# Another order for the instructions of a two-layer attention and feed-forward kernel, with a changed planner constant

## The chip, the cores and the metric

The kernel runs on one core of a Trainium2 chip. The metric is the device time of one execution in microseconds (us), lower is better. A core has engines that run side by side: PE (TensorE, matmuls), DVE (VectorE), ACT (ScalarE), POOL (GpSimd) and SP (SyncE, which here only issues transfers); PEld is the loading of a matmul's stationary operand. Transfers are issued from SP's and POOL's instruction queues, and each queue is worked through in order.

## The reference

The input x has 2048 rows of 512. Four stages follow one another, each added to its input after a layer norm: attention, feed-forward, attention, feed-forward, both times with the same weights.

```python
for s in range(n_seg):                       # 64 segments of 32 rows, one after the other
    h = concat([mem, xs])                    # 8 memory rows and 32 rows of the segment: 40
    q, k, v = h @ Wq, h @ Wk, h @ Wv         # 32 heads of 128
    p = softmax(where(mask, q @ k.T * scale, -1e9))
    o = (p @ v) @ Wo
    mem = o[:8]                              # the next segment needs it
    outs.append(o[8:])
...
h = sigmoid(x @ w_gate) * (x @ w_up)         # 512 to 1792
return h @ w_down
```

The memory rows make the segments of one attention stage a chain: a segment cannot begin before the output projection of the one before it.

## The kernel before

The program is first written down as a list of 13442 tasks and then emitted in an order that a string holds. `Kern.trace` (L1098) makes the list: after the start (weights loaded, the first blocks of x normed, their values computed by `v_pass` and `v_half` and stored to the DRAM tensor `scr`) come 70 calls of `emit_step` (L740). Step t does segment t of the first attention stage and segment t - 6 of the second, side by side in the same matmuls (80 columns, 40 of each; fewer in the first 6 and the last 6 steps). A step goes through the 32 heads in groups of six (three pairs):

- q and k (L817): 8 matmuls a head; ACT copies them to `qku` (L838);
- scores (L852), softmax on DVE and ACT (L866 to L883), transpose (L895), copies to `ptsb` (L909);
- product with the values (L922). The values come by transfer into the tile `vsb`, of which there are three, two in use by a step: rows computed early are read back from `scr` (L786), and the rows that need the memory are computed in the step itself as strips (L731), copied to `sst` and sent to `vsb` (L797). All of these are SP's, 16 or so a step, and a `vsb` is free again only after the products that read it;
- the output projection (L940); DVE writes the memory rows into the next step's input (L953, L958).

Between these PE does a feed-forward (`ffn`, L995) of 128 rows every fourth step for each stage: gate and up (L1042), tanh, down (L1065). Its weights do not fit, so they stream: `wg`, `wu` and `wd` tiles in rings of three, each 256 KB, loaded by POOL (L1034, L1035, L1059).

The class `Planner` (L178) sets the order. `add` (L202) gives each task its engine (or two that can do it), its assumed duration and latency, and what it reads and writes. `plan` (L239) decodes `SEQUENCE`: for every task its place among those not yet taken, then one bit for each of the 1573 tasks that two engines can do. Each engine then runs its tasks in that order. `replay` (L258) goes through the order once with assumed times, and three things of it reach the program: which buffer of a pool a task gets, where gaps foreseen in PE's time are filled with placeholder matmuls on zeros (`warm`, L322; emitted at L1159), and the pacing of the weight loads: a big transfer of POOL is given a matmul that has to end before it starts, the last one whose planned end lies `PACE` = 465 ns before the load's planned start (L295 to L300).

In `replay` a task starts when its engine is free and all that it waits for is done, with a latency on top: for a wait on PE 205 ns (`LAT`), and 32 ns more (`TO_PE`) if the waiting task is PE's (`gap`, L232, and the reuse of buffers, L285). The constant `TO_POOL` = 0 stands there (L183) but nothing reads it. The search that finds a sequence is not part of the kernel.

Of the kernel before, what the change touches and what calls it, by code (L numbers as in the profile page):

```python
# [1238 lines left out]
```

## Time and profile before

| what | value |
|---|---|
| median of 3 timed runs | 1776.29 us (1774.72 to 1777.69) |
| profiled execution, its own time | 1771.19 us |
| its span, first to last instruction | 1769.4 us |
| busy PE, PEld, DVE, ACT, POOL | 1750.3, 1507.4, 1228.8, 1113.9, 572.4 us |
| q and k matmuls (L817), two rows | 614.9 and 615.1 us |
| output projection (L940) | 367.8 us |
| gate and up (L1042), two rows | 172.1 and 171.4 us |
| placeholder matmuls (L1159) | 19.5 us, 69 of them |
| POOL's weight loads, issue to landing | 4.3, 4.3 and 4.1 us (median) |
| moved by DMA | 273.42 MB, 155 GB/s; 299 GB/s in the first 50 us |

The page gives busy times and the share of the span; PE's matmuls overlap, and their ends are modelled. A row of waits names who waited for whom, the total in us, how often, and the longest. In the chain that ended last, each line is a piece of time with its start and length and what it was spent on: work of an engine, a queue's issuing (SPq), or a transfer from issue to landing (DMA out<-in).

### The profile page before, as it was taken

How to read it: one execution, taken by the hardware profiler on the slowest of the kernel's cores; microseconds unless marked ns; L12 is line 12 of the kernel's file. 1: busy time of each engine (PE TensorE's matmuls, PEld its weight loads, DVE VectorE, ACT ScalarE, POOL GpSimd, SP SyncE). 2: the span in 40 equal slices, each digit the busy share in tenths (PEclk: the TensorE clock that was granted, in tenths of full speed). 3: DMA queues.
4: the chain of work that ended last, by engine and by line, in shares of the span. 5: the costliest groups of instructions: out<-in, count | busy, mean ns of one | idle time of the engine just before them, and what ended most of it. 6: DMA issues, size and time to landing. Idle time of an engine off the chain costs nothing.

```text
span 1769.4 us, 92147 instructions
## 1 busy us (share of the span) xinstructions
PE 1750.3 (99%) x40043; PEld 1507.4 (85%) x40043; DVE 1228.8 (69%) x4104; ACT 1113.9 (63%) x2938; POOL 572.4 (32%) x823
## 2 busy tenths in 40 slices
PE   9999999999999999999999999999999999999999
PEld 4588888889888888989898898988888898989887
DVE  5577777677667666776676777667767766767676
ACT  4576766667666656666665567666656666666654
POOL 5212032413333242323333242333325132342423
PEclk9999999999999999999999999999999999999999
DMA  9834355645555464545545554555547354554644
GB/s 316 294 96 133 96 168 148 190 113 155 151 148 151 141 181 134 169 117 161 155 141 158 140 173 127 149 160 161 161 124 209 110 159 116 155 171 121 185 128 117
DMA packets 135600, 273.42 MB, mean 155 GB/s; under 512 B 30754, under 2 KB 68522, under 8 KB 135194
## 3 DMA queue, kind: packets, MB, share of 16 engines
q0 software_dynamic: 55920, 180.99, 34.8%
q1 hardware_dynamic: 79274, 86.53, 16.9%
q8 instruction: 314, 5.14, 1.2%
q14 instruction: 92, 0.75, 0.1%
HBM read 221.78 MB, written 27.07 MB: 141 GB/s over the span
## 4 chain that ended last, share of the span: by engine, by line
PE 91%; DMA 4%; SPq 2%; DVE 1%; issue 1%; ACT 0%; POOL 0%; DVEq 0%; POOLq 0%; ACTq 0%
PE bank L817 32%; PE bank L940 17%; PE bank L1042 11%; PE bank L731 7%; PE bank L606 6%; PE bank L1065 5%; PE bank L922 4%; PE bank L852 4%; PE bank L895 2%; PE bank L566 1%; DMA wo_sb<-in_A_Wo_dram 1%; SPq L797 1%; DMA oxT<-in_A_x_dram 1%; DMA scr<-wg 1%; DMA vsb<-scr 1%
## 5 line engine op out<-in xcount | busy, mean ns | idle before, releaser
L817 PE MATMUL bank<-hT,wk_sb 128*128 128x80 bf16 (+3 forms) x8960 | 614.9, 198 | 3.7 <-issue 2.1
L817 PE MATMUL bank<-hT,wq_sb 128*128 128x80 bf16 (+3 forms) x8960 | 615.1, 198 | 0.7 <-issue 0.4
L1173 ACT CAST qku<-bank 128x480 bf16<-128x480 f32 (+3 forms) x770 | 381.6, 507 | 236.0 <-PE bank L817 208.4
L817 PEld LDWEIGHTS <-wq_sb 128*128 128x128 bf16 x8960 | 453.0, 99 | 27.5 <-issue 13.1
L817 PEld LDWEIGHTS <-wk_sb 128*128 128x128 bf16 x8960 | 447.0, 99 | 2.7 <-DMA wk_sb<-in_A_Wk_dram 1.7
L866 DVE TENSOR_TENSOR st<-bank,cst 40x240 f32<-40x240 f32 (+3 forms) x768 | 280.1, 368 | 152.9 <-PE bank L852 140.1
L940 PE MATMUL bank<-otsb,wo_sb 128*128 128x80 bf16 (+1 forms) x8960 | 367.8, 198 | 0.9 <-DMA wo_sb<-in_A_Wo_dram 0.9
L940 PEld LDWEIGHTS <-wo_sb 128*128 128x128 bf16 x8960 | 337.8, 99 | 12.8 <-DMA wo_sb<-in_A_Wo_dram 1.3
L1173 ACT CAST otsb<-bank 128x480 bf16<-128x480 f32 (+3 forms) x420 | 201.5, 482 | 97.9 <-PE bank L922 69.5
L1059 POOL DMA_DIRECT2D wd<-in_B_w_down_dram x217 | 154.0, 710 | 311.3 <-PE bank L1065 110.8
L1035 POOL DMA_DIRECT2D wu<-in_B_w_up_dram x217 | 164.7, 759 | 256.0 <-PE bank L1042 82.9
L1034 POOL DMA_DIRECT2D wg<-in_B_w_gate_dram x217 | 164.1, 757 | 248.8 <-PE bank L1042 122.9
L876 ACT ACTIVATE st<-st 80x240 f32<-80x240 f32 (+3 forms) x420 | 159.6, 382 | 67.8 <-DVE st L873 64.8
L1042 PE MATMUL bank<-xnT,wg 128*128 128x128 bf16 (+2 forms) x1784 | 172.1, 219 | 1.2 <-DMA wg<-in_B_w_gate_dram 1.1
L1042 PE MATMUL bank<-xnT,wu 128*128 128x128 bf16 (+2 forms) x1784 | 171.4, 218 | 0.0
L878 DVE TENSOR_REDUCE small<-st 80x6 f32<-80x240 f32 (+3 forms) x420 | 151.1, 361 | 24.9 <-ACT st L876 22.3
L852 PE MATMUL bank<-qku 128*128 128x80 bf16 (+1 forms) x2240 | 162.7, 198 | 0.9 <-ACT qku L1173 0.9
L873 DVE TENSOR_TENSOR st<-st,small 80x240 f32<-80x240 f32 (+3 forms) x420 | 154.9, 371 | 6.6
L883 DVE TENSOR_TENSOR pb<-st,small 80x240 bf16<-80x240 f32 (+3 forms) x420 | 153.7, 370 | 6.0
L871 DVE TENSOR_REDUCE small<-st 80x6 f32<-80x240 f32 (+3 forms) x420 | 151.7, 363 | 6.0
L922 PE MATMUL bank<-ptsb,vsb 104*128 104x80 bf16 x2048 | 140.6, 199 | 3.9 <-DMA vsb<-scr 2.8
L556 POOL TENSOR_TENSOR small<-small,cst 128x1 f32<-128x1 f32 (+1 forms) x80 | 46.2, 578 | 301.8 <-DVE small L555 299.9
(107 smaller groups left out, 2412.5 us busy)
## 6 DMA issues: line engine op xcount, KB each, us to landing
wg<-in_B_w_gate_dram POOLq DMA_DIRECT2D x220, 256.0 KB, 4.3
wu<-in_B_w_up_dram POOLq DMA_DIRECT2D x220, 256.0 KB, 4.3
wd<-in_B_w_down_dram POOLq DMA_DIRECT2D x220, 256.0 KB, 4.1
vsb<-scr SPq DMA_DIRECT2D x460, 48.0 KB
vsb<-sst SPq DMA_DIRECT2D x464, 32.0 KB
scr<-vst SPq DMA_DIRECT2D x112, 96.0 KB
wv_sb<-in_A_Wv_dram SPq DMA_DIRECT2D x8, 512.0 KB
wo_sb<-in_A_Wo_dram SPq DMA_DIRECT2D x10, 384.0 KB
```

Of the source, the lines that this page charges most:

```text
L817: nc.tensor.matmul(o_ap, lhsT=W[:, c, h * P:(h + 1) * P], rhs=mv(c), start=(c == 0), stop=(c == DC - 1))
L852: nc.tensor.matmul(s_all(SB)[:, w0 + i, :], lhsT=fview(qku[:, i, 0, 0:1], [(1, P)]), rhs=qku[:, i, 1, 0:ncol], start=True, stop=True)
L866: pl.add("DVE", dve_ns(n, True), lambda gsz=gsz, hs=hs, st=st, SB=SB, pj_=pj_, npj_=npj_, mk=mk, idx=idx: nc.vector.tensor_tensor(out=st[p ...
L873: pl.add("DVE", dve_ns(n), lambda gsz=gsz, hs=hs, st=st, mx=mx: nc.vector.tensor_tensor(out=st[pr, hs], in0=st[pr, hs], in1=mx[pr, hs].uns ...
L876: pl.add("ACT", act_ns(n), lambda hs=hs, st=st: nc.scalar.activation(out=st[pr, hs], in_=st[pr, hs], func=ACTF.Exp, scale=self.scale), r=s ...
L922: nc.tensor.matmul(fview(OB[:, o:o + 1], [(ncol, 2), (1, L)]), lhsT=self.vsb[halves[u // 8]][0:64 + L, j, (u % 8) * P:(u % 8 + 1) * P], rh ...
L940: nc.tensor.matmul(WB[:, c * ncol:(c + 1) * ncol], lhsT=self.wo[:, h, c * P:(c + 1) * P], rhs=otsb[:, hl, 0:ncol], start=(h == 0 and c == ...
L1034: pl.add("POOL", 760, lambda wg=wg, fs=fs: nc.gpsimd.dma_start(out=wg[:], in_=self.wgv[:, :, fs]), r=[("wo", self.H - 1)], w=[gk] + bt, la ...
L1035: pl.add("POOL", 760, lambda wu=wu, fs=fs: nc.gpsimd.dma_start(out=wu[:], in_=self.wuv[:, :, fs]), r=[("wo", self.H - 1)], w=[uk] + bt, la ...
L1042: nc.tensor.matmul(gu[:, 2 * i + k, 0:n], lhsT=W[:, c, i * P:(i + 1) * P], rhs=xnT[:, c, rw], start=(c == 0), stop=(c == DC - 1))
L1059: pl.add("POOL", 760, lambda wd=wd, ip=ip: nc.gpsimd.dma_start(out=wd[:], in_=self.wdv[:, 2 * ip:2 * ip + 2, :]), w=[dk] + (["boot"] if se ...
L1173: nc.scalar.copy(out=dst, in_=src)
```

## The change

Two things change. First, the planner: `TO_POOL` becomes 257, and a new method reads it, so that in the planned times a task of POOL that waits for PE counts 257 ns more.

```diff
-    TO_PE, TO_POOL, PACE = 32.0, 0.0, 465.0
+    TO_PE, TO_POOL, PACE = 32.0, 257.0, 465.0
...
-        return a.lat + d + (self.TO_PE if b.eng[0] == "PE" else 0.0)
+        return a.lat + d + self.over(a, b)
+
+    def over(self, a, b):
+
+        return self.TO_PE if b.eng[0] == "PE" else self.TO_POOL if a.eng[0] == "PE" and b.eng[0] == "POOL" else 0.0
...
-                        t = max(t, ready(T[u], tk, 0.0 if same else T[u].lat + (self.TO_PE if tk.eng[0] == "PE" else 0.0)))
+                        t = max(t, ready(T[u], tk, 0.0 if same else T[u].lat + self.over(T[u], tk)))
```

Second, all lines of `SEQUENCE` are others (85 before, 84 after, some 14,000 characters). The tasks, what they depend on and what they compute stay; their order on each engine and the engine of some copies change:

| read out of the two strings | before | after |
|---|---|---|
| tasks on PE | 4202 | 4202 |
| tasks on DVE | 4100 | 4132 |
| tasks on ACT | 2937 | 2905 |
| tasks on POOL | 812 | 814 |
| tasks on SP | 1391 | 1389 |

Of the 1573 tasks that two engines can do, 530 change engine. PE's order differs mostly in where pieces of the feed-forward, values and scores lie between the projections of a step; in 50 of the 70 steps the last output projection has the same matmuls' work ahead of it within 0.05 us. In SP's and POOL's queues the transfers of a burst stand in another order.

More of the change, by code (lines that the diff above doesn't have):

```diff
@@ new lines @@
+@_r#~~-gm}MW;UejiWp{aJ)hi+l<6Ygrtd;7TKwO!xBySu(XZCrMjF7u`VA8t(jR!J{zR48z@Aiz$Lx>u=+Da|Nd@Jl@C!f9e6$s2{=Bom3p1|oAKY+p+<pV&Q?LU`v_4TZTh(Y*7k{uTw~)t889>{(ro!SoMr>PYU15#msZ
+_}t+ek9rur<9#IIr?bpIJH!kkm1`@DI$;_#upVyKMH=^*}z36l&bjqmxJr<2*;@Y&`>sORISXA?*4Kh9}6>clU~Q*(Ztx-1Jo^LiJ>2)99=JGEZs{pR9wj?m6fv{5u6yJ=7B^Cg2-DU*XDS*q4ueJ*wl#L0OuF3gnn2@I2W|
+I|9NbCrGR{Jip%xBqiFuV!Bf$3M6;LjF=W~UJH<g7`i1VZsE@R51DQH=IuLCb0}H4MUuI$tk4{EQMv@7i|pXc7{od_bJ!Z;@A?LZUj6-~nJg^Vw(q5xhy>fv4)%eRgl;}7W1feO6xvgFOVo@{Q<g$S!T41ZYWD8X{RWev3Zy
@@ new lines @@
+Ryh1AKtZJ}*M_d~*clQv!?_O(LhFXy4^Qy{g%b)re${{`K14VW+80jW^+%|bLlIPN{3#$&3*iV$hcYnMKO!1J+2V2B1-?Nwzxa@r+Mm#a>F?%b_X0C(3ljxJ!j7@`4ot+NL;c>g(MRO9?aJFC3a2Ho_!g$sV{WYL?Dkal!XV
+@+^^eEU8<s#XnQjX*dw-{8J<gnvo|+_`w`?W7wu&vlEO%YqB(OaA}fFr87cMohwR1MpZ^*xOT0#NJhLsn&T>0d5v<eo!!}8XV9CdnF=U9mjeEnL!4(d7yZ_ybuRghPRU61x0_vQN?a;z1ZW7fSPMM?R0|&Xal0odTIy)MUXz
+!bvxg-Ou0A5;&?tJxBc#?w=~3THxeKX1EHJ+?AzCG1r?&dIc$K9BsxIj9Zcc#LFncBB%GRpQ)KxBVCx|g-ENCrklW{MH*^IEXc_4`1V-jREC${Q3`gH*^=;P7?|&0H+hM>-HkZ{W%ztPn=z^-pEI7t?>6h+vGqOr6Rvuy4ft
@@ new lines @@
+40nPc@$uPvEosQ2Y|)nIKXK&rh{I&Uox}Xp@l}ND@z;eQp@H`^4M?0si?|>FM7a?7yYnOurV4#EoGevdai_XMK~SBs;eeQ5~(9z-V({bt18AG~n!isTDl8Msk-c0ADjgC0C3*@Lwuq0C>(sD}rOMj{g`;D(bSEs)wuVmckUp
+47ma*F*bKwFl>YscB(?TVKo(g3kksEi%iB^E1;z@>i7Q%vz8u+FW?iy<}5d+I3sgF%xP^!tZnw|V-q;3=hAT82qj4r&re;vxN)T-GCRM$yI3WX!~7VHvgH!`8$?Y}G%kFMxT7_r*m89mwn(T&iKVdqcbmG|hgSzj_5|g{OJc
+R(5d9!S3u|k+d&!DQb-K44Pe7Y`5o#evpE&KVqp*p4myYjmV`Gd3d{OPFkFJ*f=l;RVz1IB+&uXZK%RxX1!}UsW5X1gnspCdb`l4k*4T(kICd;vH3Zyr~Eq5|)@v=}{IAR{b+8@TVaS$JT+H&`VT<A*-9$4)n2zyJt+TqV^%
@@ new lines @@
+&r8W@^zu2WI>;NZiq15vYQx0;<C)fwd-H1a-`+j`h7}-l3x1|C9g`OGsFGRJN2yvDUU^Kx7u%@nR*J!6forss36zR+~{<;1WM(#<emy&6Jk$&m?iDL7Tt1<*)QN?B0mQ~3gQ+tNr{~(0b`g4<9N<DmOQEtE9G?A&A9q@Z3+`
+#@HHeP5*_V#W%tQF#8^3A@APVUvQb0w=$uax&HuCqWt{+-5wWpr4@v{s-GYDc^^df-s41ZzUxpa{uQtm>FNGR!{g5n-VUB|x2@eZC>;+ubkKjE3D>|FuN;&;f@@Zs4MwdCIwVhk#=2eawi%w8jh$O(XZ{5TJk!25T4pgdm#m
+zm54B6Y{`mGUuXP3*KW0w-P)f)#nXX@|I%cdQTW4tUYmtjn`()Uj3zf4HoC=Em|0y~KitYRDX24EI`drN7z>9+(;&Q^CzHl1#J=;DP{?QfsTEI+}7I3^z#zt>mq>j>+t_?66QS1nXMY@Ad_=HTt2jFm8~wA60Dvbny8*u3CN
@@ new lines @@
+8XmnU?X+LwX3ui2zXnF`bSu+yn5T>7>HT2<GC(Z5pXRTMs8w`PC)?$nA`3?3oz-KmdaQ(;env^f8ps5q7lkRR14}KCC_Mn2jAAn>TdiihS&6`L!3u_e6IYY62rL=CFm`8@T(gS^rBAYX<|x~<2RPtw`4{~KQOJ5GHc$W}Y`i
+RRZg;<&k{>$m$cuPAft<?N+IN}Vahdk5Q+39I?~+x7E0~X0qV(0-T1l@{jg+^S@`^Bl%4!l}TCayYFH6GRY8?{1vu3oPUVbY74a2#l2r8Xg50WFBwe(4nGfp+799}_x-JxrZ5RMv<ciRxtB2;k6dDuo4>0zxTtyRY^+KE~<i
+Y7eAJ3J{5XDKorFD&=Nbp{3pDcYUlE*1Go1~q@8ilQQ6I{-q!Z)KHnVYIV?3F9r!IdpY$NBlUNS}U5r8S3)IqMesa1o?qe)u&ujG6qY$<K|2mHo3)fU&RN&s5e_K7O{=_9z6UkN2K9ViA^krjvD$Irv;^oiMEUlbI-=G*Fp|
+)3lv(5@bmv6cKn`3?%<$pV}@=g&$a@nlS=nHJZgg2)AlXrc*mV!#bQ(%j(}7p{wKV7Q7e*!pVj0WQ*OEEgKiaV8TV5+)?P7Y=y)P@lkOCdGucw4MhU|(y_Z~%W3TJGeTs#8Z&87JcrRX6(b>2pz0W>V|3}`d3{CRTSfQ;fNC
@@ new lines @@
+u%8OyxIJ89R~d<fCY3jx=~fe%avFoU-+!EP4A-)7Q7hl%Ak<D?&|yAD?78YFi=Ac$dc1K>5Mp(vOcS8u-P<_+}J^I3dWDopUxmaB~dOpw@l+>AUfT%Lm+Z4_XU@#p5|93`O^5+4{PHUPyDfasia4jqzozHQ6IHVAr|pHp1OV
+mr!C?Dt8(P0bHn3oPsfsUZyANxTC-WGyIxKf}sEVJo{x*1A4O`O3Q<6YM9zEKRPeNZ^-nCG%z|oN;}h1PV2mVONn6Do_z+E90fa8`6s4t67mjA25kEvYYqo)6Jz|@kWdDOWHynvJraE`0gKYEnak+p#fPw;1qKRHk5Ou}(Sn
+V78>^6>fFK2PqQ!(4_pN{&{C<s-n!<+1Vu#NOZf6z4wW3gqVMlBM`Vy>KnmLBZ_b4cYwMJj!P_p#FxX^SeZbO0|ac2YW)}8m*|N63&qv@DOra9i@?5l*njGHeZY9zmBwxku>Atv2FYO{ZHgDCof$X`@$subc&<5thxNrEePt
@@ new lines @@
+AudIJfh2W!CdP_KLPV5>~6>mN=!JEjZ_^?Y4!p<>BDvZL+O<jN@f00Mu1b^hSWR~6@mm4O7_>Gcc&a7X$#2Fw$)a)5L-Z314z8D+I0KfCFsQ+=2?YpWLhK#y{2Ia!JS+=Lm6mTw2xO;3FHvm5`34FeI-#B@A2z?wYX=ARxw_
+tuU8@k{fr{Sv#bo>Ks?jgSsjAv`4DFOKn#VKjcu1tDl6w&PU|^<tJP?A&5l$ttcM6ID_N9j;;<WhQiw4_LXSBOeX11wz`70FI;cFy8~DROxYvx`b@MGwNs#1bU&pyd#a+<Xs3R#iO52d=-AB*d#Y^Aso1Jez3|PMaRj#COH;
+j$tHfy;ya4~ZKc>T=`3oJwkZeD=T;z@<u{owk44ldXh%2iR6r&W231gX5+c0{M)49=*|_YDUr6-f~?YYbz0>pb}X5N5;XR0uSqAoxgU&`4^zJ}AFvfTW-Jl^DejXZ%iCCo_fxf4)pQY^8L6vDJ$x!?4Q;NqOKdbR}llga}&Q
@@ new lines @@
+@eZf>iaIQTN$S6A1e(DeM3KXW9R$jeJRw**TZS_+ZHJ0SCKRm;RU(r?51y~gO#_UJ=AvfX<CODs?AzSp#2@Jw8Weh;`Xw05k|8w%kWeWBkb(PDladC&@8Xi_At?H$TVx_1VDRzcNW#H3=pPLqZ{@V;3r6^idU9=U2QDycoCa
+}X<;9E#ct(Zl!i5Ah`!104t8F2UlGY-aWLUe36yGaoQi9HIJIS~ZBtpEL_gL{cRne-!yMVsnL%kUF1tjZNAA(o!hj4mte1`ZPSs_ZWjP25@@Xc*@bg|<JslWe(&UFAz{yV(Lc&=-k{l0+Rw(aML&yWGi@U=v05n!X~4dEHN3
+m95IPR`Aoo1;&d;XHy#!rlQZy}j#{(5htjIUq?0uP)lrfl7+`Xt4^f&W((|J(a!~11KdUbe3#G9ecttYzELIl@`Y_t-(t<57??;gSqPhA~-b$>FH;;&G8u6xHN+)OAn_aeS74l%s`TV1#otgP4`uCbaYkS*$wYD#-JIqA_P0
@@ new lines @@
+#1J5g+)l8UK7?&!3NizPK&S215c-|HTih11x?l3$m)#n7wLgw-7oQ#IyuKGzx8WyOf+DtpQ&s%y&PD(|r#(rw@s?44YCP$bJ0Po<HriBC3R~Qq|dRO-XA8y9ZQfC%)osl)<i&be@gKqatZK>(u4_|U@U<WWn#-tE*68Zi+<~
+;sa1ky6+J{9Vj*YtYD3Tt)pzA^(E|HNwv6y2U8ZsLTHjF|=Zf#%6UkV<WLhOd;+Z1&F`_)t8ROVo_&EahI7xPY-GgQ(!n!|W=fn`Il6EGc?ngbb8FQ7?@xKhnyoC_e-?&*%>hY+>=|4yCasgBKR&8H+%LzD~kzqWwfXGsqD*
+?1%6y!A8@Td&;#;U^SZ1^N`4T@)Z&3;oK(flk;5-c^%X^j!*~r4YY=jW5m#XE$QyDcWw*LEx%fv895eWw7Yg_JAe2rJhkz{ATZ&QGu`;*diH=ydnsA$BkIXPb^6p~(mz<j7rz9^k15#?N#N6qQKskAG85E>aB`r-2shNeRov
@@ new lines @@
+e=IMOZvfHg1t?EQ(of^BmUiwl<K!np`>y0se`d%^yn?f9+=kDcWb)XlTYcB~xTMlN@*-|wXZjJ%ki&MXd8-&bsOEoA5Mh=p+pjF^;rf~#WB@#nMKrVD!xV7&4&D1n8$nFJ&CGe;C$wyV=SHb)RQ7O_q|Q@xx{Ps>4B3)h|6Y
+Z4*#cO$R)(t|Z|z<zv}FKZijIBcTHKjMi%CzRpCI;@mBit1}-SlP!sowvv`H!5$|qNK5RR*#~^EJtME+S!-vgll!5;7j9of>#1|$&IV(q0}(K0)sQ=4LW!&MFa&r0;Uxeu;;mC!|cEZnU*bjIQ&f{yTR-xadAP_4Ib+^s95P
+558E(H5{&c2T7Vlh;oarLxWPacTwuKjuWPWSE}sFh(-J#V*T0QX`*Ar=g60>)+ZiXR>?W_ToSBx{&14#k;wm;Iu8@EosGYaBl$*NdM|rPTgeaoTEr?vIU*H`xIid@#h=%j@<6HkDB+Kn}-98p0+e?4=Z5CRdv6CB_XbTjB5U
@@ new lines @@
+i;}kKO-8kmg>@5<06G+sXnrIg9gV*mMFaZ5)2%F#q|fSNs8rv%-FcJ}LT<AyXtgYqV9~kUlxD{K_<Z5OVN0wLP?r0w+o4$Ze}~=Z9EMT7=yafzJusmAclbmz9TVpx~#`vb~@c{6GCIPz#{5y{+O6O50(IMNCIX+QI|IW_&SO
++te<Jgv>W3qhxtF<GhYBL?nVPgR|y>D>OZ})C3O_v;K<xYY~YB4pMPJ!saxrKUBmxQT)=o-U{cLdZO_U*uJPcA~$ypL_N#}E(GsT5!;fM;qOw=rP4MLGNYpawv#r=L}xfb_!<o(0__lO$V$<rWtLQKeML$J9(H0D5b@okfJm
+LES-?xAA)ICmEgnLGL2Ul!9UZy@y*WXTv3Bp$1h-JP+cOEo>%Ghw39pQz(Hl|z@B6F`#Z&Q!Ff*#RIk|5#J~^mcX*5LeCV^p@j}JGOh3ppQeYTcZh##M1<W&f6*NS+K$<MymH5=zc|9)(`tWuiH>qc;C0s(g4ydoAm9ocdsu
@@ new lines @@
+;LR{N_AMqOq=@oM8DrR!sgqeF-~OAjvL4g!KI6e9EACK@~P*agJEaZcW~e4_g&w{EC031XLA70canUmHw@;xlOwboX6=wI@uapuHXE@9rZ}xZU#sn=%?P28Jd(X;oxMRenVnh^aq58De*FrUhT#$8Ze8~j$V%L+Y8SbR?c+7
+Z#4_9Ze)n&=%)B9--_JpaimP1;FuCL1#!tCui?Y7;ocEmktl;)FYiKOz)R#;1RAHC;eR29gRrS-S{bIuNOxeoCn<BQ$tmbGFmKmANEb@O9=Ygqp+=ImkN?T;Oc?>fEm@LsGkuJy{3zYwQs@lnOTs1a^3FzYDfoz&Vs^Zmf{>
+;>pp_mo7DJ5s4U~tlD`EC6<9m8$QSg?avq59L1S~Bv7w54MR3?$roWel+*c+#5N32_StS<|WhnK>XowbHXmAfQm*-XUY8hGQJRKFvg)Pw1HLCt!=mpp6zVv-tp(rEnQYbg_%zUX+@@{R(_gmDolu3KKHH3r`(T_z*{N8=VrA
@@ new lines @@
+#5^o2td_E)Gh&vJyBwFP5mG631|UN2le{`l6!>&1t~PiE{kEZ|Ho}f@y@W7{OPQC{dpR?sk8_c72tT>UnZ}dk8!xv5CyCidpIwTQ(R%s}R(&=#Hd*#(J60srdqHBaR<NGi;*r8tDhV28{~tCo!ZT`YTG_NJ)dhT)%$)^nvh<
+b)v{BiSl4WnQd~Fv6g`vp^_Y4VD^%AkG0rom;muP^hlmXA)SuVfdNcfYoOVWs4@)eSDJ^lIOvKwFEO~E+)g(qZhg}XQGA%GRvvnh1$Q3SGdAts`WURE*utvM*zTmQ^K3?9Mmc6je@dO4b#usAJFP8ixexKGIa;!l;j1sV8Kk
+g8;)3PQnS{QE1pjhq)$q?Uv0&DsMI^6ij^PW*nrxbJ(8PCp#+Z3>e>n=vd(d(e`6nEx4mAT<0I24tGIU(L7S{OBM{Zj{=u>uADpkA_-_v}=$ssW%j)0w579+UF&0EN4_S=k&kfl7JLoUkJDW4Rp<`<CmX6s=CgN`DLKa8%hu
@@ new lines @@
+#Vhbv~fBrd^5hp$apsJdYf3N;vlUu+yfR$wbbZqFpc(@}wuo5oTy!y?VKEwn)Oz*~wN4HJlI~cabjA74}m>WFiA4IelBJW@NzPT*4Muq&yz?NDMXEkfG&9wIW3PjO+u`bauq*R*SquDYJGNU=sAEzlE3*xEqY2?pm8RUR%>=
+MY88rp-K>B3z`{V~L&r5ooHnqHkkjRsMgj59{%3KVq7Nhpvn1>X9lT8UtwefRYnv$Rg%idDP-&}~)79Cn?ww>~e_xNb<A%%;I`DJVf)-@KytAl5g9Krr<?{)W{G#b}C;P*H(#Gn?UXQ5J`d7OH$rP-I`zamqMN3*D>4(#_!*
+qN@mh^*6lW783>nt~jtnka*LbEF^y5#go+7qV;&A>&hCkU1d=!_F@A=R>Id0{}7uWp@aJ|8*Ui(ah7(|vdw%-(JkvqgeXLA;$k5;?FNwJpW?-8Ga^!WrrA2MgV1*%7955F2RK&5;&FA@qh7p_v6}_wultW9#VCfGBZF~hH$J
@@ L139 @@
+msPqstrFg<;^uWX{vO(TY#6U5StaFUzA&X|3gE)#qdr(GJWtGiE%ibx<YI$LvGGkbHBKThgBkpx|W&q!d;J;$A#mdGh9{39EojQ`fXx;n^G_)PI(q3RYOx$3SqLGHm9dYryO0!LezG|>?!5m=rAJm2O;hA$XtHQ2kyK)g%Qb
+NC?TkoXhVAbrEHdzqgE-A>_Ab0(V$jHAyo|^veTSWGe#Ny^D)T%=l9eXeB^iNJ%mXRF8nk8&o;vucVGY
 """
```

124 lines of the change are left out of this document (39 added, 85 removed).

## The prediction

> **What bounds the kernel now.** I read the page first, then the waits of PE, then the chain and SP's timeline around the longest wait that is no start-up wait.
>
> ```profile
> span 1769.4 us, 92147 instructions
> PE 1750.3 (99%) x40043; PEld 1507.4 (85%) x40043; DVE 1228.8 (69%) x4104; ACT 1113.9 (63%) x2938; POOL 572.4 (32%) x823
> ...
> DMA  9834355645555464545545554555547354554644
> ```
>
> PE is at 99%, DVE and ACT have 540 and 655 us free, and the DMA engines are full only in the first two slices (9 and 8 tenths, 88 us). All matmuls stay, so the change can only touch the 19.1 us in which PE is idle, the 19.5 us of placeholder matmuls (L1159, written into gaps that the planner foresees at the start), and time lost to a lower clock. A gain over some 15 us is not there to be had. Who ends PE's idle time:
>
> ```profile
> PE bank L922 <- DMA vsb<-scr: 2.8, 2, 2.1
> PE bank L817 <- issue: 2.5, 3, 1.4
> PE bank L606 <- DVE xvf L1175: 1.7, 1, 1.7
> PE bank L817 <- DMA wk_sb<-in_A_Wk_dram: 1.6, 1, 1.6
> PE bank L1042 <- DMA wg<-in_B_w_gate_dram: 1.1, 1, 1.1
> ...
> PE bank L922 <- DMA vsb<-sst: 1.0, 2, 0.8
> ...
> PE bank L940 <- DMA wo_sb<-in_A_Wo_dram: 0.9, 2, 0.6
> ```
>
> Columns: total us, times, longest. Transfers that land late (vsb, wk, wg, wo) make 7.4 us, in eight waits out of 1391 transfers of SP and 715 of POOL. Between 300 and 900 us the rows of 50 us show PE at 50.00 in all but one: there is nothing to win there but what is lost in other executions. The longest late transfer, from the chain:
>
> ```profile
> 941.09 0.51 SPq L797
> 941.60 0.04 issue
> 941.65 4.97 DMA vsb<-scr
> 946.61 0.25 issue
> 946.86 0.47 PE bank L922 x6
> ...
> 948.84 1.60 PE bank L940 x24
> ...
> 952.56 0.86 PE bank L940 x24
> ```
>
> Step 36's first attention-value product needs a transfer that SP issued at 941.65, the last of 16 that it issued without a pause from 931.80 on; it landed 4.97 us later and PE sat idle 2.1 us. Then the same 24 matmuls that take 0.86 us take 1.60. The windows say why:
>
> ```profile
> 946.86:950.00 3.14, 3.14 (x56) 3.11 (x57) 1.23 (x4) 2.44 (x7) 0.79 (x1) 0.74 0.13 50
> 950.00:958.00 8.00, 8.00 (x166) 7.53 (x164) 3.13 (x11) 3.34 (x9) 4.50 (x6) 0.89 0.68 189
> ```
>
> The third number from the right is the granted clock. 3.14 x 0.26 + 8.00 x 0.11 = 1.7 us were lost to it: half clock for 3.4 us. So one late transfer cost 3.8 us, 0.2% of the span. [...]
>
> **The constant.** TO_POOL gives 257 ns more, in the plan, between PE's last read of a weight tile and the load that refills it. On the chip no wait comes of it: the load waits for the tile's readers (unchanged) and for a pacing matmul that ended 465 ns before the planned start. With the start at 205 + 257 ns after the last reader, the pacing matmul ends 462 - 465 = 3 ns before that reader's end (2 with the 1 ns that L298 allows), so it still comes no later. Where the planned transfers or POOL's own queue set the start instead, it can start up to 0.26 us later, against 0.39 us and less of extra distance (next part). Cost: 0, bounds -0.3 and +0.3 us in all. The 69 placeholder matmuls can change where foreseen gaps do; those are start-up gaps, costed with the start-up.
>
> **The sequence.** The string holds, task by task, the place among those not yet taken, and one bit for each task that two engines can do. Read out of both strings over the same 13442 tasks: matmul work ahead of each step's last output projection is equal within 0.05 us in 50 of 70 steps and differs by 0.9 us at most; 1093 of PE's 4202 tasks have the same work ahead, 3172 are within 1 us. So the skeleton stays. 266 copies go from ACT to DVE, 234 back: 32 more on DVE at some 0.5 us (the mean of the cast row of L1173 is 507 ns) are 16 us of DVE's 540 idle, and as much less on ACT. They lie beside PE; without that cover they would cost those 16 us, but PE's waits for DVE and ACT together are under 5 us now and the chains from qk to score, from transpose to product and from product to projection have the same work between (medians 1.72 against 1.83, 1.52 against 1.51, 1.40 against 1.40 us). 0, bounds -1 and +1 us. 16 start-up stores go from SP to POOL and 14 back.
>
> What is really moved is the order of SP's and POOL's queues inside the bursts. I count the distance of a transfer: the matmul work in PE's order (36 ns for 80 columns, 216 for 512) from what releases it to the matmul that needs it, less 0.55 us for each transfer queued behind that on SP (the timeline shows 0.51 to 0.59) or 0.75 on POOL (0.70 to 0.79). The four late ones after the start-up:
> - 946.86 (2.1 us idle, 1.7 us clock): the reload moves from place 787 of SP's queue to 755; the shortest distance of what this product needs goes from 4.6 to 10.6 us.
> - 1554.75 (0.8 us): strip transfer issued at 1551.12, landed 3.50 us later; 4.3 to 7.7 us.
> - 226.19 (1.1 us): the wg load that the feed-forward needs first is the sixth of a group of loads issued from 209.33 on, at 221.18, and lands 4.96 us later; in the new order it is the first of the same group.
> - 291.14 (0.7 us of the 2.8): landed 3.96 us after its issue; shortest distance 4.9 before and after. It stays.
>
> So **what goes**: 2.1 + 1.7 + 0.8 + 1.1 = 5.7 us.
>
> **What is late next.** In steps 14 to 63 the products that have a transfer with a distance under 5 us are 26 before and 13 after (under 5.5: 46 and 24; under 6: 60 and 43). The 26 gave two late ones worth 2.1 + 1.7 + 0.8 = 4.6 us; 13 should give half, **+2.3 us**. For the ring of weight tiles the shortest distance from last reader to next goes from 6.8 to 7.2 us (wg, wu) and from 6.1 to 6.4 us (wd); with landings of 4.3 and 4.1 us none was late in the steady part, so this brings nothing in this execution.
>
> **Start-up.** The first value weights have one x block (131 KB) less ahead, 0.4 us at 299 GB/s (the first 50 us). But the wk load that PE waits for at 63.70 has as many bytes ahead in SP's queue as before (15.3 and 15.4 MB), so what is won ahead of it is waited for there. The last wo pieces have 0.2 MB less ahead, 0.7 us, against 0.9 us of waits for them: I take **-0.5 us**. The four 917 KB loads of wq and wk now stand behind stores whose matmuls end about 23.7 us, the first of the four was issued at 20.11: bounds -2 and +3.6 us.
>
> **Sum.** -5.7 + 2.3 - 0.5 = -3.9 us on the profiled execution, 1771.19 us (span 1769.4 and 1.8 around it): 1767.3. The median of the three timed runs is 1776.29, 5.1 us above the profiled one; nothing that I have shows in what. If nothing of that changes, 1772.4; if it is late transfers, halved like the 26, 1769.9. I take the middle, **1771.2 us**.
>
> **Rivals.** (1) Late transfers are chance and distance hardly matters: other transfers take the place of the four, and only the start-up's 0.5 us stays, 1775.8 us. For it: 24 of the 26 tight products waited for nothing, and the 2.5 us of "issue" waits belong to no transfer. Against: all four waits had their last transfer at the end of a burst. [...] Here the burst took 9.85 us to issue and the last transfer 4.97, so I hold it unlikely.
> (2) Slower: the new order's own tight places. The reloads of the third head group in steps 50, 30, 18 and 26 have 3.5 to 3.8 us; landings of late ones took 3.5 to 5.0 us. If these land at 5.0, PE waits about 1.3 us there and, where that costs the clock, 1.7 more: 4 x 3.0 = 12 us, in place of the +2.3: 1781 us. It decides from a landing of some 4 us after issue. Against it: in the old order step 18 has 3.3, step 30 3.6, steps 22 and 46 3.7 us, and no PE wait stands there.
>
> **Chances.** A measurement of this kernel tells some 0.2% (3.55 us) from no change; faster is below 1772.74, slower above 1779.84. My forecast 0.57, the first rival 0.25, the second 0.18. The forecast's own range is 1766 to 1773; with the rivals and the start-up's bounds 1765 to 1781.
>
> **What would show it.** Right: no wait of L922 over 1 us in steps 36 and 60, no wg wait near 226, clock 1.00 in every row but the end, DMA rows of PE's waits after 130 us under 3 us together. Wrong: new vsb waits at the tight steps with clock rows under 1.00; the wk or wo wait of the start-up longer; or waits gone from the profile and the timed median unmoved, which would mean that the 5.1 us lie elsewhere.

## The result, and the profile after

The changed kernel took **1766.12 us** (median of 4 runs, 1764.51 to 1766.95), beside the kernel before with 1775.51 us (1773.10 to 1777.69, 4 runs) on the same chip: ratio **0.9946** with a 95% interval of 0.9929 to 0.9964, 9.4 us or 0.54% faster. The forecast was faster, 1771.2 us: the direction held, the change was about twice what I said, and the time lies at the low end of the range that I gave, 1766 to 1773. How much of the mechanism held is asked below. The two profiled executions, however, differ by 4.2 us (1771.19 and 1766.95; span 1769.4 and 1765.1), where my sum said 3.9. The profiled execution of before was faster than its three timed runs then (1774.72 to 1777.69), that of the changed kernel the slowest of its four. The rest of this document asks where the 9.4 us lie, and why one pair of profiles shows half of them.

All line numbers are 3 higher after the change: L820 is q and k, L925 the product with the values, L943 the output projection, L1045 gate and up. Three lines of the page after:

```profile
span 1765.1 us, 92070 instructions
PE 1735.9 (98%) x39831; PEld 1505.6 (85%) x40045; DVE 1244.9 (71%) x4136; ACT 1103.3 (63%) x2906; POOL 573.8 (33%) x825
...
DMA  9935364644555464545556464555456553554544
```

DVE's busy time rose by 16.1 us and ACT's fell by 10.6, as the 32 copies say; no long wait of PE shows it. PE's busy time must not be compared: this trace has 39831 matmul records beside 40045 weight loads, so some are missing. What ended PE's waits, from the list of waits (total us, times, longest):

```profile
PE bank L820 <- issue: 3.0, 5, 1.0
PE bank L943 <- DMA wo_sb<-in_A_Wo_dram: 1.3, 1, 1.3
PE bank L820 <- DMA wk_sb<-in_A_Wk_dram: 1.0, 2, 0.8
...
PE bank L925 <- DMA vsb<-sst: 0.9, 3, 0.4
```

The row of wg is gone, and no wait of the products for a transfer is longer than 0.4 us. Step 36, where before PE sat idle for 2.1 us at 946.86 and then ran at a lower clock, in the chain after:

```profile
942.71 0.06 issue
942.76 0.38 PE bank L855 x6
943.14 0.22 PE bank L925 x6
943.35 0.90 PE bank L1045 x16
944.25 0.22 PE bank L925 x6
944.47 0.86 PE bank L943 x24
```

The first product comes right after the scores, and 24 matmuls of the projection take 0.86 us, not 1.60. The stretch of 100 us around it in three kernels, first before, then the old order with the new constant (`old_257`, below), then the changed kernel; the third number from the right is the granted clock:

```profile
900.00:1000.00 100.00, 97.94 (x2183) 86.34 (x2180) 68.55 (x224) 59.56 (x147) 30.96 (x44) 0.98 0.49 140
```

```profile
900.00:1000.00 100.00, 99.25 (x2264) 88.42 (x2276) 72.21 (x237) 62.58 (x155) 33.45 (x46) 1.00 0.51 147
```

```profile
900.00:1000.00 100.00, 99.11 (x2261) 88.27 (x2271) 72.31 (x233) 63.25 (x157) 32.18 (x45) 1.00 0.52 148
```

The second of them matters: the same order as before, and no lost clock. The event of step 36, two thirds of what my sum removed, is a draw that one execution had and another had not. So it is in good part luck that the profiled pair came out as I had summed it.

**Steps as a ruler.** DVE's write of the memory rows ends each step, so its times can be laid side by side in eleven traces. (Two executions far longer than all others of their kernel, one of before at 2459.86 us and one of `old_sp` at 2154.85, ran at a granted clock of 0.65 and 0.75 and are in no ratio; `old_sp`'s trace is of the second.) Us from the span's start to the end of step 5, then the length of three parts (start order is that up to step 12, middle that of steps 13 to 62):

| kernel | start order | middle | to step 5 | steps 6-12 | steps 13-62 | rest |
|---|---|---|---|---|---|---|
| before | old | old | 174.1 | 172.6 | 1270.4 | 152.3 |
| old_257 | old | old | 174.0 | 172.6 | 1264.5 | 152.0 |
| old_sp_2 | old | old, SP's queue altered | 174.5 | 172.3 | 1266.3 | 151.8 |
| mid_new | old | new | 175.5 | 172.6 | 1265.5 | 152.8 |
| start_new | new | old | 177.0 | 170.6 | 1268.1 | 152.2 |
| ends_new | new | old | 173.9 | 170.2 | 1267.2 | 150.4 |
| after | new | new | 174.8 | 169.7 | 1266.8 | 153.8 |
| new_again | new | new | 172.0 | 169.8 | 1265.7 | 152.7 |
| new_0 | new | new | 173.3 | 169.8 | 1267.0 | 150.8 |
| new_up | new | new, SP's queue altered | 173.4 | 170.5 | 1266.9 | 152.7 |
| new_sp | new | new, SP's queue altered | 174.6 | 170.3 | 1274.8 | 155.0 |

Only one column separates the orders in every trace: steps 6 to 12, 172.3 to 172.6 us with the old start and 169.7 to 170.6 with the new. The stretch to step 5 and the rest scatter by 5 us whatever the order. The middle scatters over 5.9 us with the old order (four traces) and over 1.5 us with the new (four). The shortest middle of all is an old one that nothing disturbed (1264.5 us): in these traces the new order does not make the middle shorter, it makes a longer one rarer.

### The profile page after: what moved, and what is told of

Its sections match the earlier page's. It is cut to its first block, busy times and chain, and to the rows that moved or that the text cites. A ratio compares the mean times of both kernels' runs of the same rounds, so it can differ in the third digit from the quotient of the medians.

```text
span 1765.1 us, 92070 instructions
## 1 busy us (share of the span) xinstructions
PE 1735.9 (98%) x39831; PEld 1505.6 (85%) x40045; DVE 1244.9 (71%) x4136; ACT 1103.3 (63%) x2906; POOL 573.8 (33%) x825
## 4 chain that ended last, share of the span: by engine, by line
PE 89%; DMA 4%; DVE 3%; SPq 2%; issue 1%; ACT 1%; DVEq 0%; POOL 0%; ACTq 0%
PE bank L820 31%; PE bank L943 17%; PE bank L1045 11%; PE bank L734 7%; PE bank L609 6%; PE bank L925 4%; PE bank L855 4%; PE bank L1068 4%; PE bank L898 2%; DMA wk_sb<-in_A_Wk_dram 1%; SPq L800 1%; DMA vsb<-sst 1%; PE bank L569 1%; SPq L496 1%; DVE st L869 1%
## 5 line engine op out<-in xcount | busy, mean ns | idle before, releaser
L820 PE MATMUL bank<-hT,wq_sb 128*128 128x80 bf16 (+3 forms) x8960 | 615.7, 198 | 3.0 <-issue 1.8
L820 PE MATMUL bank<-hT,wk_sb 128*128 128x80 bf16 (+3 forms) x8960 | 615.5, 198 | 2.5 <-issue 1.2
L820 PEld LDWEIGHTS <-wq_sb 128*128 128x128 bf16 x8960 | 452.7, 99 | 32.3 <-issue 17.1
L820 PEld LDWEIGHTS <-wk_sb 128*128 128x128 bf16 x8960 | 447.0, 99 | 3.1 <-issue 1.8
L943 PE MATMUL bank<-otsb,wo_sb 128*128 128x80 bf16 (+1 forms) x8960 | 362.8, 198 | 2.4 <-DMA wo_sb<-in_A_Wo_dram 1.3
L943 PEld LDWEIGHTS <-wo_sb 128*128 128x128 bf16 x8960 | 334.6, 99 | 11.1 <-DMA wo_sb<-in_A_Wo_dram 1.4
L1045 PE MATMUL bank<-xnT,wg 128*128 128x128 bf16 (+2 forms) x1784 | 171.7, 218 | 1.0 <-issue 0.2
L1045 PE MATMUL bank<-xnT,wu 128*128 128x128 bf16 (+2 forms) x1784 | 171.2, 218 | 0.2 <-issue 0.2
L925 PE MATMUL bank<-ptsb,vsb 104*128 104x80 bf16 x2048 | 140.6, 199 | 3.3 <-DMA vsb<-sst 0.9
L1051 DVE SCALAR_TENSOR_TENSOR hff<-th,bank 128x256 bf16<-128x256 f32 (+2 forms) x231 | 93.0, 403 | 62.8 <-ACT th L1049 62.3
```

The lines of the kernel that those rows point to most:

```text
L820: nc.tensor.matmul(o_ap, lhsT=W[:, c, h * P:(h + 1) * P], rhs=mv(c), start=(c == 0), stop=(c == DC - 1))
L925: nc.tensor.matmul(fview(OB[:, o:o + 1], [(ncol, 2), (1, L)]), lhsT=self.vsb[halves[u // 8]][0:64 + L, j, (u % 8) * P:(u % 8 + 1) * P], rh ...
L943: nc.tensor.matmul(WB[:, c * ncol:(c + 1) * ncol], lhsT=self.wo[:, h, c * P:(c + 1) * P], rhs=otsb[:, hl, 0:ncol], start=(h == 0 and c == ...
L1045: nc.tensor.matmul(gu[:, 2 * i + k, 0:n], lhsT=W[:, c, i * P:(i + 1) * P], rhs=xnT[:, c, rw], start=(c == 0), stop=(c == DC - 1))
```

## The experiments

My theory: what was won is late transfers, and a transfer is late, now and then, where the order leaves little between its landing and its use. Rivals, with the letters of the expectations: (A) another part of the order brings the gain (other engines' shares, PE's own order); (B) lateness is chance and the place in the queue hardly matters; (C) the constant does; (D) the gain lies at the start and the end, not in the middle. For the later runs I replaced the distance of the prediction by the **planned margin**: the planned start of a PE task minus the planned landing of the last transfer that it needs, as `replay` has them. Of the products of steps 13 to 62 the old order has 13 with a margin under 0.5 us and 37 under 1 us, the new order none and 9 (planned with the new constant; the kernel before, planned with its own, has 9 and 34). Unless said otherwise the kernels have the new constant. Ratios are to the kernel before on the same chip. Line numbers differ by kernel: the product with the values is L922 before, L925 in the changed kernel, and L916, L920 or L921 in the others.

**The constant alone, and the sequence alone.**

```diff
 old_257: sequence of before
-    TO_PE, TO_POOL, PACE = 32.0, 0.0, 465.0
+    TO_PE, TO_POOL, PACE = 32.0, 257.0, 465.0
```

> The old sequence with the new planner code and constant (257). Only the pacing matmuls of the weight loads change: 153 of 672 loads wait for a matmul one to three PE tasks later. Theory: within 1.5 us of before, as the prediction's zero has it. Rival C (the later weight loads collide less with SP's transfers, and that is the gain): 3 us or more faster.

```diff
 new_0: sequence of the changed kernel
-    TO_PE, TO_POOL, PACE = 32.0, 257.0, 465.0
+    TO_PE, TO_POOL, PACE = 32.0, 0.0, 465.0
```

> The new sequence with the constant back at 0: 164 of 672 weight loads wait for a matmul one to three PE tasks earlier. Theory: within 1.5 us of the new kernel, 1764.5 to 1767.5. Rival C: 3 us or more slower than the new kernel.

`old_257` gave 1.0008 (0.9995 to 1.0021), `new_0` 0.9963 (0.9951 to 0.9976). The constant by itself does nothing that can be measured, the sequence does it: rival C falls. Whether 257 adds something in the new order, as the 0.9946 of the first comparison might say, the overlapping intervals do not tell.

**SP's queue in another order altogether.**

```diff
 old_need: order and constant of before; SP's queue, steps 13 to 62
-1391 transfers in the order found
+984 of the places changed: always the one whose product comes first in PE's order
```

> The kernel before with one edit: in steps 13 to 62 SP's queue is put in the order of need (of the transfers that are released, the one whose product comes first in PE's order goes first). PE, DVE, ACT and POOL keep the old order. Products with a distance under 5 us fall from 27 to 11 (13 in the new kernel). Theory (late transfers are what the old order loses, and the place in SP's queue makes them late): 5 to 8 us faster than before, near the new kernel. Rival A (the gain is in the order on PE, DVE and ACT): within 2 us of before. Rival B (late transfers are chance): within 2 us of before.

```diff
 new_oldSP: changed kernel; SP's queue, steps 13 to 62
-1389 transfers in the order of the changed kernel
+919 of the places changed: in the order in which the kernel before has them
```

> The new kernel with one edit: in steps 13 to 62 SP's transfers stand in the old kernel's order (919 of 1389 places differ). Products with a distance under 5 us rise from 13 to 26, under 3 us from 0 to 9 (step 42, 46 and 26 mostly). Theory: 5 to 10 us slower than the new kernel, at 1771 to 1777, with waits of L925 for vsb at steps 42 and 46. Rivals A and B: within 2 us of the new kernel, 1764 to 1768.

1.2235 (1.2214 to 1.2256) and 1.1603 (1.1582 to 1.1625), far outside every expectation. In `old_need` the page has, of its groups of instructions, the first line below; the chain has the second, and SP's own waits the third:

```profile
L1153 PE MATMUL bank<-hot 128*128 128x512 bf16 (+1 forms) x1934 | 428.7, 377 | 1.4 <-DVE small L460 1.0 <-ACT kx L1167 0.4
```

```profile
425.30 8.42 PE bank L1153 x39
```

```profile
SPq L780 <- PE bank L916: 619.8, 90, 21.4
```

L1153 is the placeholder matmul there: 1934 of them, 428.7 us, against 69 before. SP waits for products to free a `vsb` while it holds back what other products need; the planner foresaw these gaps and filled them: by `replay` the planned spans are already 2156 and 2042 us, against 1745 for before. My distance had left out that a transfer also has to wait for its buffer. Both runs say that SP's order can cost 16 to 22%, and nothing on how late landings divide the gain; the later kernels keep to what the plan allows.

**Only some transfers, with the planned span unchanged.** A local search moved single value transfers in SP's queue; the order of all other engines and the planned span stayed.

```diff
 old_sp: order of before; SP's queue, 217 of 1391 places changed, value transfers pulled forward
-products with a planned margin under 0.5 us: 13; under 1 us: 37
+products with a planned margin under 0.5 us: 5; under 1 us: 19
```

> The old order on PE, DVE, ACT and POOL; in steps 13 to 62 single vsb transfers are moved ahead in SP's queue (217 places of 1391 differ), so that by the planner's times products whose transfers land less than 0.5 us ahead of them fall from 13 to 5, less than 1 us from 37 to 19 (the new order: 0 and 9). No planned gap is added. Theory: 1 to 3 us faster than before and fewer executions under clock 1.000. Rival A (order on the other engines): within 1 us of before.

> The kernel before with 217 places of SP's queue changed (attention-value transfers pulled forward; planned margins under 0.5 us 13 to 5, under 1 us 37 to 19), once more for a profile that can be read. First time 0.9979 [0.9964, 0.9993]. Theory: 0.997 to 0.999 again, and no wait of the attention-value products over 1 us in steps 14 to 62. Rival (chance): 0.999 to 1.001.

```diff
 new_sp: changed kernel; SP's queue, 261 of 1389 places changed, value transfers pushed back
-products with a planned margin under 0.5 us: 0
+products with a planned margin under 0.5 us: 31
 e.g. step 44, a transfer that the first product needs, and that product's margin
-place 941, margin 2.79 us
+place 950, margin 0.03 us
```

> The new order on PE, DVE, ACT and POOL; in steps 13 to 62 single vsb transfers are moved back in SP's queue (261 places of 1389 differ), so that by the planner's times products whose transfers land less than 0.5 us ahead rise from 0 to 31 (old order 13), without a planned gap. Theory: it loses the gain, 4 to 10 us slower than the new kernel, with waits for vsb in the profile and clock under 1.000 in half of the executions. Rivals A and B: within 1.5 us of the new kernel.

`old_sp` gave 0.9979 (0.9964 to 0.9993), and once more, as `old_sp_2`, 0.9967 (0.9953 to 0.9981): 3.7 and 5.8 us for earlier places in one queue and the constant, which alone gave 1.0008. The trace of `old_sp_2` has two waits for value transfers in steps 13 to 62, 0.8 and 0.2 us; executions under clock 1.000, of which I had expected fewer, were 8 of 11 in `old_sp` (19 of 34 of before on that chip) and 2 of 8 in `old_sp_2` (17 of 25). `new_sp` gave 1.0006 (0.9993 to 1.0020): the whole gain is lost, and 11 of its 12 executions are under clock 1.000. Its trace shows where. The last two rows of SP's timeline in the burst of step 44, then three pieces of the chain:

```profile
1146.01 0.49 SPq L784 DMA_DIRECT2D vsb<-scr  x1
1146.54 0.51 SPq L795 DMA_DIRECT2D vsb<-sst  x1
```

```profile
1146.54 4.84 DMA vsb<-sst
1151.38 0.04 issue
1151.42 0.44 PE bank L920 x6
```

And the windows around it (length, busy time of PE, PEld, DVE, ACT, POOL, then the granted clock):

```profile
1148.00:1151.40 3.40, 0.54 (x13) 0.41 (x10) 1.13 (x4) 0.42 (x2) 0.00 (x0) 1.00 0.45 146
1151.40:1155.00 3.60, 3.58 (x42) 2.79 (x43) 2.74 (x9) 2.05 (x6) 1.48 (x2) 0.71 0.18 36
1155.00:1163.00 8.00, 8.00 (x178) 7.52 (x177) 4.37 (x16) 4.64 (x13) 2.98 (x4) 0.92 0.51 141
```

It is the event of step 36 made on purpose, at the product whose margin I had cut to 0.03 us: last in its burst, landed 4.84 us after its issue, PE idle for 2.9 us, then 3.60 x 0.29 + 8.00 x 0.08 = 1.7 us of clock lost. The step is 4.7 us longer than that of `new_0`. Steps 13 to 62 took 1274.8 us, 8.5 more than the mean of the four undisturbed new ones (1266.3). The two waits for value transfers and the clock are 5.3 of these; 2.0 are waits that the profile puts to "issue", whose cause is open. Rival B falls, and A with it for the middle: moving SP's transfers alone, with every other engine's order kept, gave 3.7 and 5.8 us in the old order and took the whole gain from the new one. (`new_sp` goes further than the old order, with 31 tight products where that has 13.) The last transfer of this burst took 0.51 us to issue and 4.84 to land. But the 16 issues of step 36's burst took 9.85 us, and moving issues within one queue was worth 0.4 to 0.6% in `new_sp`, so in this kernel, where the queue issues in bursts, the place counts.

A small margin makes a late transfer possible, no more: 31 products stand under 0.5 us in `new_sp`, and PE waited for value transfers twice in steps 13 to 62 of this execution (2.9 and 0.8 us); the first product of step 45, at 0.20 us, did not wait.

**More margin than the new order has.**

```diff
 new_up: changed kernel; SP's queue, 254 of 1389 places changed, value transfers pulled forward
-products with a planned margin under 1 us: 9; under 1.5 us: 30; under 2 us: 51
+products with a planned margin under 1 us: 8; under 1.5 us: 15; under 2 us: 34
```

> The changed kernel with 254 places of SP's queue changed: transfers of the attention-value products of steps 13 to 62 pulled forward by up to 14 places, so that fewer products have a planned margin under 1.5 us (30 to 15), under 2 us (51 to 34), under 2.5 us (83 to 58); under 1 us 9 to 8. Order of every other engine and planned span unchanged. Theory (what matters is the number of products with a small planned margin): those under 1 us are nearly the same, so 0 to 2 us faster than the changed kernel, ratio 0.994 to 0.9965. Rival (distance hardly matters): the same as the changed kernel within 0.1%. A result slower than the changed kernel by over 2 us would speak against both.

> The changed kernel itself once more, beside the others. Its first comparison gave 0.9946 [0.9929, 0.9964] from four executions; its sequence with the old constant gave 0.9963, and the gains of its middle (0.9985) and its ends (0.9976) add to 0.9961. If the sequence is all, this should come out at 0.9955 to 0.997 (5.3 to 8 us). A ratio under 0.995 would say that sequence and constant together give something that neither gives alone.

`new_again`, the changed kernel once more, gave 0.9950 (0.9934 to 0.9965): 1763.33 us against 1772.44 us, a little more than the 0.9955 to 0.997 that I had expected. `new_up`, on the same chip, gave 0.9963 (0.9949 to 0.9978): not 0 to 2 us faster than the changed kernel but 2.0 us slower by the medians, just where I had said that a result would speak against theory and rival both; the intervals overlap. In these steps more margin from about 1 us on brings nothing that can be measured; its profile has no wait for a transfer at all in steps 13 to 62, and that of `new_again` has one, of 0.2 us. No version here beats the changed kernel.

**Which steps.**

```diff
 mid_new: order of before,
+but the changed order from step 13 to the end of step 62
 ends_new: changed order,
+but the order of before from step 13 to the end of step 62
 start_new: changed order to the end of step 12,
+the order of before from there on
```

> The old order to the end of step 12 and after step 62, the new one between. Theory (the median's gain is late transfers in the long middle, which come at random and cost a clock window each): 4 to 6 us of the 6.5 to 9.4 us gain, and executions with a mean clock under 1.000 rare (13 of 32 in the old order, 1 of 13 in the new one). Rival D (the gain is in the start, where the old order waits for a wg load at 226 us, for wo and for x, and in the end): 0 to 2 us.

> The new order to the end of step 12 and after step 62, the old one between. Theory: 1 to 3 us faster than before (the wg wait of 1.1 us and what the start gives), and executions with a clock under 1.000 as frequent as in the old order, about 4 in 10. Rival D: 5 to 9 us faster.

> The new order to the end of step 12 and the old order from there on, with the new constant. The kernel with new order at both ends gave 0.9976 [0.9966, 0.9987], 4.2 us. In the profiles the new order gains 2.2 us at step 8 (the wg wait), about 1.1 at step 10, 2 in steps 0 and 1, and loses some 2.5 in steps 2 to 7; at the end it gives some back. Theory: the gain of the ends lies here, 3 to 5 us, ratio 0.997 to 0.9985. Rival: it lies at the end of the program, then 0.999 to 1.0005.

`mid_new` 0.9985 (0.9973 to 0.9997), `ends_new` 0.9976 (0.9966 to 0.9987), `start_new` 0.9971 (0.9959 to 0.9982): 2.7, 4.2 and 5.1 us. The first two lie between what my theory (4 to 6 and 1 to 3 us) and rival D (0 to 2 and 5 to 9) asked for. The gain is in both parts, and by the medians the larger share, not the smaller as I had thought, is in the start, though the intervals overlap; what lies after step 62 brings nothing that shows. Start and middle together, 5.1 + 2.7 = 7.8 us, come near to the whole (8.9 and 9.4 us).

In the start it is steps 6 to 12, by the ruler (2.4 of the 5.1 us), and in these steps 8 to 12. PE's waits between 219 and 349 us in `mid_new`, whose start is the old one:

```profile
PE bank L921 <- DMA vsb<-scr: 1.5, 1, 1.5
PE bank L1041 <- DMA wg<-in_B_w_gate_dram: 0.4, 1, 0.4
```

These two, of step 10 and of step 8, stand in all four traces with the old start, 1.3 to 1.9 us together, and in none of the seven with the new. The new start has a small one of its own in step 7, a `vsb` transfer that comes 0.3 to 0.9 us late, in every trace; its planned margin is 0.11 us, and steps 6 and 7 are some 0.7 us longer. Which queue or engine removes the two old waits no run takes apart, so for the start rival A stands. In the middle it is step 60 as well as step 36. PE's timeline in `ends_new`, whose middle is the old one:

```profile
1549.23 0.34 PE L921 MATMUL bank<-ptsb,vsb 104*128 104x80 bf16 x5 [1.74 <-DMA vsb<-sst]
```

The same product waits in `start_new` (1.6 us) and waited in before (0.8 us), and not in `old_257`. Of the four traces with the old middle three have waits for transfers over 0.7 us there (2.1 and 0.8, 1.7, 1.6), of the four with the new middle none (the longest 0.6).

## Why the prediction came out as it did, point by point

**The constant: nothing.** Right, 1.0008.

**What goes.** The event of step 36 (3.8 us) and the wait of step 60 (0.8) are gone from every trace with the new middle. In the old order their planned margins are 0.40 and 0.56 us (0.63 and 0.56 with the constant of before), in the new 5.3 and 3.7. I booked them as certain in before and gone after; `old_257` has neither. In the profiled pair step 36 is 4.1 us shorter (29.7 and 25.7), which is why the sum of the pair came out; but in `old_257`, with the old order, it is 3.9 us shorter too. The wg wait of step 8 (planned margin 0.03 us before) is there every time and is gone, as said.

**291.14 stays (0.7 us).** Wrong: it is in all four traces of the old start and in none of the new. The distance was 4.9 us in both orders, and the planned margin is no larger in the new one (1.7 against 2.1 us), so neither measure saw it: here 2.1 us of planned margin did not keep a transfer from being late every time. What in the order removed it was not isolated. Steps 6 to 12 are 2.4 us shorter (means 172.5 and 170.1) where I had 1.1. The two waits are 1.3 to 1.9 us of that, the new wait of step 7 takes some 0.6 back, and the plan itself, whose times my prediction left out, has these steps 0.7 us shorter.

**What is late next, +2.3 us.** Too high. In the traces with the new middle the waits for transfers in steps 13 to 62 sum to 0, 0.3, 0.2 and 1.9 us, 0.6 in the mean. The half of the tight products that remain by my distance have planned margins of 0.58 us and more, and `new_up` shows nothing to be won by more.

**Start-up, -0.5 us.** Nothing to be seen: to step 7 the old start took 219.6 to 221.2, the new 218.2 to 223.5 us. One of my signs of being wrong did appear, a longer wait for wo (0.9 us before, 1.3 after), but over the eleven traces this wait goes from 0 to 1.7 us, whatever the order.

**DVE and ACT: nothing.** No wait for them that matters stands in the profile after. No run tried it alone.

**The median's excess: the step that failed.** Of the 5.1 us between before's median and its profiled execution I took 1.2 us away, the middle between "nothing" and "halved". The median came down by 9.4 us and the profiled pair by 4.2, so 5.2 us went beside the sum. Some of it can be estimated. A granted mean of 0.999 for a whole execution is about one loss of clock as in step 36 (1.7 of 1767 us). How many executions have one differs by chip, so I set kernels beside before on the same chip. On one, 17 of 25 executions of before were under 1.000, by 1.16 thousandths in the mean, and 3 of 6 of `new_again`, by 0.50. On another it was 5 of 20, by 0.30, and 1 of 9 of `new_0`, by 0.11. At 3.8 us for an event, idle time and clock as in step 36, and one event for each thousandth, the differences are 2.5 and 0.7 us. With the 2.4 us of steps 6 to 12 that makes 4.9 of 9.1 us and 3.1 of 6.5. The counts do not divide cleanly by part: `mid_new` has 3 of 12 and `ends_new` 4, where before had 19 of 34, and `start_new` has 5 of 12, where it had 17 of 25. The other 4.2 and 3.4 us I could not place, and their cause stays open. The measurement itself is that coarse: the interval of `new_again` is 6.2 to 11.7 us.

One rival no run takes apart: by `replay` the new order is itself shorter, 1742.8 us against 1744.9 (1746.1 with the new constant), and only 0.7 us of that lie in steps 6 to 12. In the middle this did not arrive: planned 1.6 us shorter than with the old order, it took 1265.5 to 1267.0 us, where the undisturbed old one took 1264.5.

**The rivals.** That lateness is chance was half true: each event is a draw. But the odds hang on the order, and `new_sp` shows it (3.6 us of waits for transfers in steps 13 to 62, against 0 to 1.9 in the traces with the new middle). The slower rival, landings of 5 us in steps 50, 30, 18 and 26, did not come: with the new middle no wait for a transfer in steps 13 to 62 is over 0.6 us, as long as SP's queue is left as it is.

## What to carry to other kernels

Where one engine is at 99%, look at what the planned order leaves between a transfer's landing and its use: places with some tenths of a us (0.40 and 0.56 at steps 36 and 60) were late here in some executions only (in before, not in `old_257`), so one profile shows a sample of them, and a sum over one profile can miss what removing them all is worth; here the pair of profiles shows 4.2 of 9.4 us. Lay several traces of one kernel side by side, by a mark that each step has, before calling a wait systematic; and take the margins from a replay that knows the buffers, because a queue order judged by need alone cost 22% here.

## What the runs showed of the hardware

After a single idle stretch of 2.1 us (before), 2.06 us (`start_new`, up to 25.60) and 2.9 us (`new_sp`) the granted clock was lower each time: 0.74 and 0.89 in the two windows from 946.86 on, 0.57 from 25.60 to 29.00, 0.71 from 1151.40 to 1155.00. After stretches of 1.74 us (`ends_new`), 1.6 us (`start_new`) and 1.5 us (`mid_new`) in the steady part it was 1.00 in the windows that follow. The window after the one in `start_new`:

```profile
25.60:29.00 3.40, 3.40 (x49) 2.30 (x50) 0.25 (x1) 0.62 (x2) 0.00 (x0) 0.57 0.88 325
```

The length of the gap alone does not decide it: `new_0` lost the clock at the start after one of 1.6 us (granted clock 0.78, then 0.73), and `old_257`, which has one of 2.0 us there, shows 1.00 over its first 50 us. In before, the stretch at a granted clock of 0.50 and the one of the same length ahead of it are these:

```profile
944.98:948.39 3.41, 1.53 (x32) 1.53 (x33) 1.42 (x6) 0.88 (x3) 0.73 (x2) 1.00 0.51 148
948.39:951.81 3.42, 3.42 (x52) 3.42 (x49) 2.54 (x8) 2.12 (x6) 1.54 (x2) 0.50 0.40 111
```

The clock fell 1.5 us after PE had taken up work again (946.86 and 948.39), and PE had been busy for 1.53 of the 3.41 us ahead of that. What decides whether an idle stretch of some 2 us costs the clock the runs do not show.
